# A planned attention kernel: more shifted copies by transfer, a constant row from VectorE, an epsilon add on GpSimd, other thresholds of the planner

## The chip, the cores and the metric

One core of one Trainium2 chip runs the kernel. Five engines work from instruction streams of their own: TensorE (PE; its weight loads stand apart as PEld), VectorE (DVE), ScalarE (ACT), GpSimd (POOL) and SyncE (SP, which here only issues transfers). The metric is the time of one execution on the device in microseconds, as the median of the timed runs; lower is better.

## What is computed

Four layers on one sequence of 2048 rows of 512 numbers (bf16): two attention layers (A), each followed by a linear-attention layer (B), with a layer norm ahead of each and a residual around it. A has 32 query heads of width 16 that share one key and one value head.

```python
def _A_ref(x, wq, wk, wv, wo):
    q = (x @ wq).reshape(B, S, H, Dh).transpose(0, 2, 1, 3)
    k = x @ wk
    v = x @ wv
    scores = jnp.einsum("bhqd,bkd->bhqk", q, k) * (Dh ** -0.5)
    p = _softmax(scores, axis=-1)
    o = jnp.einsum("bhqk,bkd->bhqd", p, v)
    return o.transpose(0, 2, 1, 3).reshape(B, S, H * Dh) @ wo

def _B_ref(x, wqkv, wo):
    q, k, v = split(x @ wqkv)
    phi = lambda t: jnp.where(t > 0, t + 1, jnp.exp(t)) + 1e-6
    pq, pk = phi(q), phi(k)
    kv = jnp.einsum("bhsd,bhse->bhde", pk, v)
    den = jnp.einsum("bhqd,bhd->bhq", pq, pk.sum(2))[..., None] + 1e-6
    o = jnp.einsum("bhqd,bhde->bhqe", pq, kv) / den
    return o.transpose(0, 2, 1, 3).reshape(B, S, D) @ wo

x = A_x
x = x + _A_ref(_layernorm(x), A_wq, A_wk, A_wv, A_wo)
x = x + _B_ref(_layernorm(x), B_wqkv, B_wo)
x = x + _A_ref(_layernorm(x), A_wq, A_wk, A_wv, A_wo)
x = x + _B_ref(_layernorm(x), B_wqkv, B_wo)
```

## The kernel before

**The order is planned ahead.** The program does not write its instructions down in order. While it is built, a class `Planner` plays an event simulation: each operation has a duration, a latency and a priority, an engine takes the ready operation with the lowest priority number, and the order in which they were taken is written out as that engine's instruction stream. On the chip each engine works through its stream strictly in order and waits at semaphores. So a duration or a threshold in the planner costs nothing by itself; it changes which instructions there are, and in which order they stand.

**Blocks of attention.** The 2048 rows are 16 tiles of 128. A layer A has 16 query tiles x 2 halves of the heads x 16 key tiles x 4 row groups: 2048 blocks of 128 keys x 512 query columns, so 4096 in the two layers. For each block PE computes scores into a PSUM bank (L958; two to four blocks run side by side in PE's rows), somebody takes the exponential, and PE multiplies the result with V (L1012; up to four blocks side by side in PE's columns). The exponential has two ways:

- **ACT**: one activation (L1134) over two or three banks, bf16 into a buffer (PT, or borrowed space in xnT and OBB). The block needs one product with V.
- **DVE**: a scaled score becomes, by one add and a maximum into int16 (`dve_take`, L1215), the bits of a bf16 power of two with a linear mantissa. To smooth it, the block is used four times (`NSH = 4`), shifted by 0, 1, 2 and 3 quarters of an octave and weighted: four products with V, the shifted weights standing in VW. Four blocks form a chunk of 128x2048 in a buffer (FB, or borrowed space in OBB, sacc, xn, wq and wo2), and three further buffers take the shifted copies. A shift is one int16 add over the chunk (`dve_shifts`, L1263).

**Copies by transfer.** One of the three copies of a chunk, that for shift `DSH = 1`, can be made without DVE. A generator `prime` loads a free buffer with a constant row from DRAM (`cst`, named shift_row; a transfer of 512 KB from SP's queue, L1283), keeps up to `NPRE` such buffers, and `dma_shift` issues from POOL a transfer that adds the chunk onto the buffer (`accum_op=ALU.add`, L1292). `dve_shifts` uses it if the chunk is full, a primed buffer is there, the segment is not among the last `DMIN`, and the planner's transfer path, `pl.dmaq`, is less than `DQ` us behind. The path is modelled as one queue: an adding transfer occupies it for `DXF`, a load for `DPF`, and each lands `DTAIL` later; `PGEN` is the time for which POOL is held by an issue. A load starts only while more than `FBP` buffers are free.

**Thresholds.** `TUNE[0]` is put over the defaults when the first A layer begins, `TUNE[2]` when the second does, and what neither names stays as it was left. `BLO`, `BLT`, `BLS` and `DXB` are limits on DVE's planned backlog for giving it a block; `CHT` and `ENDL` say how far ahead of ACT's place a block for DVE must lie; `AHEAD` and `FBS` hold a chunk's copies back while buffers are short; `FBO` is how many buffers must stay free before a new chunk is opened; `STICK` is the margin in priority by which PE stays with its present kind of matmul (rows or columns); `LAG` is a look-ahead of DVE and ACT in the B layers. Where PE has nothing ready, short matmuls without use are inserted (fillers: `fill`, L1057).

**Layer norm.** `ln_tile` computes for each tile mean and variance (L810, L811), adds epsilon (ve, L812, on DVE), raises to -0.5 on POOL (rs, L814) and normalizes on DVE (xn, L817). xn is transposed by PE, or for tiles that are not urgent by a transposing transfer from SP's queue (L736, planned at `DTL = 4.0` us). VW comes from POOL (L861). In program order POOL's stream holds these small operations and the issues of the adding transfers, one behind the other; SP's holds loads, transposes and stores.

**The constant row** is made at the start by a POOL memset of a whole FB buffer (L691), and its first partition is stored to DRAM (L692).

Of the kernel before, what the change touches and what calls it, by code (L numbers as in the profile page):

```python
# [7 lines left out]
FP32 = mybir.dt.float32  # L8
I16 = mybir.dt.int16
ACTF = mybir.ActivationFunctionType  # L10
ALU = mybir.AluOpType

PE, AC, DV, PO, SP = "pe", "act", "dve", "pool", "sp"
ENGS = (PE, AC, DV, PO, SP)

P = 128
S, D, H, DH = 2048, 512, 32, 16
T = S // P
# [325 lines left out]
class Seg:  # L344
# [11 lines left out]
    def take(self, js, back=False):  # L356
# [22 lines left out]
LAG = 0.15  # L379
# [16 lines left out]
BLS = 1.4  # L396
BLO = 5.0
DXB = 2.0
BLT = 2.5
# [11 lines left out]
ENDL = 12  # L411
NSH = 4
# [6 lines left out]
FBO = 2  # L419
FBS = 4  # L420
AHEAD = 20
CHT = 19
PSH = False
STICK = 1.5
# [3 lines left out]
DSH = 1  # L428
DMIN = 4
NPRE = 2  # L430
PGEN = 1.1
DPF = 2.5
DXF = 4.5
DTAIL = 2.5
DQ = 4.0
FBP = 6
TUNE = {0: {"FBS": 5, "AHEAD": 15, "LAG": 0.15, "ENDL": 12, "FBO": 0, "BLO": 7.0, "DXB": 1.6, "BLT": 3.2},
        2: {"FBS": 3, "DXB": 1.6, "ENDL": 9, "BLS": 1.0}}


def bass_interleave_layers__grouped_kv_mqa__linear_attn_block__prompt_kernel(
# [12 lines left out]
    op = pl.op  # L454
    sb = nc.alloc_sbuf_tensor
# [18 lines left out]
    xn = sb("xn", [P, NXN, D], BF16)  # L474
    st = sb("st", [P, T, 2, 6], FP32)
    mv = sb("mv", [P, T, 2], FP32)
    ve = sb("ve", [P, T], FP32)
    rs = sb("rs", [P, T], FP32)
    mhalf = sb("mhalf", [P, 1], FP32)
    ident = sb("ident", [P, P], BF16)  # L480
    mask8 = sb("mask8", [P, 8, 17], BF16)
# [11 lines left out]
    NFB = 12  # L493
    FB = sb("FB", [P, NFB, CHB * 512], BF16)
# [179 lines left out]
    def pool_op(fn, writes, reads=(), dur=0.2, prio=0.0):  # L674
        return op({PO: (dur, fn)}, reads=reads, writes=writes, prio=prio)
# [10 lines left out]
    cst = nc.dram_tensor("shift_row", (1, CHB * 512), I16, kind="Internal").ap()  # L686

    def fb_keys(i):
        return [("FB", i, h) for h in range(CHB)]

    pool_op(lambda e: e.memset(FB[:, NFB - 1, :].bitcast(I16), DSH * 128 // NSH), fb_keys(NFB - 1), dur=1.2, prio=8.0)  # L691
    op({SP: (0.54, lambda e: e.dma_start(cst, FB[0:1, NFB - 1, :].bitcast(I16)))}, reads=fb_keys(NFB - 1), writes=["cst"], prio=8.0, lat=2.5, dma=True)  # L692
    pool_op(lambda e: e.memset(kmask[:, 1:2], KSC), ["kmask"], dur=0.1)
    for j in range(4):
        for r, v in ((0, KSC), (1, 0.0)):
# [42 lines left out]
    def until(*keys):  # L738
        for k in keys:
            yield ("ops", pl.ws(k))  # L740
# [60 lines left out]
    def ln_tile(L, t, prio, far=False, crit=False):  # L801
# [6 lines left out]
        else:  # L808
            n = 1
            op({DV: (0.6, lambda e: e.bn_stats(st[:, t, 0, :], x_sb[:, t, :]))}, reads=[("x", t)], writes=[("st", t)], prio=prio, lat=0.13)  # L810
        op({DV: (0.09, lambda e: e.bn_aggr(mv[:, t, :], st[:, t, 0:n, :]))}, reads=[("st", t)], writes=[("mv", t)], prio=prio, lat=0.13)  # L811
        op({DV: (0.07, lambda e: e.tensor_scalar(out=ve[:, t:t + 1], in0=mv[:, t, 1:2], scalar1=1e-5, scalar2=None, op0=ALU.add))},  # L812
           reads=[("mv", t)], writes=[("ve", t)], prio=prio, lat=0.16)
        op({PO: (0.55, lambda e: e.tensor_tensor(out=rs[:, t:t + 1], in0=ve[:, t:t + 1], in1=mhalf[:], op=ALU.pow))},  # L814
           reads=[("ve", t), "mhalf"], writes=[("rs", t)], prio=prio - 9.0)
        i = yield ("acq", xn_pool, prio)
# [132 lines left out]
    def run_a(L):  # L949
# [324 lines left out]

        def prime():
            yield ("flag", ("K", L, T - 1))
            yield from until("cst")
            while state["si"] < len(segs) - DMIN:
                if len(primed) >= NPRE or len(fb_pool.free) <= FBP or fb_pool.wait:
                    yield ("sleep", 0.2)  # L1280
                    continue
                g_ = yield ("acq", fb_pool, 9.0)
                o = op({SP: (0.54, lambda e, g_=g_: e.dma_start(fbs[g_].bitcast(I16), cst.to_broadcast([P, CHB * 512])))}, reads=["cst"], writes=fb_keys(g_), prio=9.0,  # L1283
                       lat=0.2, dma=True, behind=guest(L, "FB", g_), xfer=(DPF, DTAIL))
                primed.append((g_, o))
            while primed:
                g_, o = primed.pop()
                pl.give_after(fb_pool, g_, [o])
# [607 lines left out]
```

## Time and profile before

| what | value |
|---|---|
| timed runs, median (lowest to highest) | 1501.41 us (1501.35 to 1501.43), 3 runs |
| profiled execution, on the device | 1502.7 us |
| its span in the profile | 1501.0 us |
| granted clock of TensorE | 1.00 |
| busy: PE, DVE, ACT, POOL | 94%, 95%, 97%, 11% |
| transfers | 128.76 MB, mean 86 GB/s |

The span runs from the first to the last instruction of the profiled execution; what lies around it makes its device time 1.7 us longer. Busy time is the union of an engine's instructions. On ACT and DVE an instruction's record overlaps the start of the next one, so that the mean of a group is longer than the time for which it holds the engine. Fillers on PE count as busy. The stages, by the share of busy time: 0 to 50 us start, 50 to 700 the first attention layer (with parts of the first B layer inside it), 700 to 850 the rest of the first B layer and the start of the second attention layer, 850 to 1450 the second attention layer, then the end.

### The profile page before, as it was taken

To read this page: it belongs to the slowest core of one execution; us is meant where nothing else is said; L and a number is where in the kernel's file an instruction comes from. 1 tells how busy PE (TensorE), PEld (TensorE's weight loads), DVE (VectorE), ACT (ScalarE), POOL (GpSimd) and SP (SyncE) were. 2 spreads that over 40 slices of the span, in tenths; PEclk is the share of its full clock that TensorE was granted. 3 is DMA by queue.
4 is the path that set the end of the run, shared out by engine and by line. 5 is a ranking of instruction groups with operands and counts; after the bars stand their busy time and mean duration, and the time that the engine had idled before them with its cause. 6 is when DMAs were issued, how large, how long until landed. Compare 5 with 4: busy or idle time off the path is not lost.

```text
span 1501.0 us, 36621 instructions
## 1 busy us (share of the span) xinstructions
PE 1418.2 (94%) x14634; PEld 514.3 (34%) x14745; DVE 1426.3 (95%) x2684; ACT 1453.6 (97%) x1519; POOL 167.2 (11%) x230
## 2 busy tenths in 40 slices
PE   7999999999999999999999999999999999999998
PEld 4433333332232233323744332333332332323335
DVE  8899999999999999998867799999999999999997
ACT  7999999999999999999799999999999999999996
POOL 5100101101010100000111101111111111100001
PEclk9999999999999999999999999999999999999999
DMA  4624533433443434001000124446464674552001
GB/s 107 176 65 114 124 65 92 106 89 78 104 104 66 92 93 89 30 15 58 2 2 1 30 51 106 111 120 152 116 152 111 151 157 108 134 131 58 16 2 57
DMA packets 71738, 128.76 MB, mean 86 GB/s; under 512 B 37521, under 2 KB 44177, under 8 KB 71570
## 3 DMA queue, kind: packets, MB, share of 16 engines
q0 software_dynamic: 14832, 54.01, 19.2%
q1 hardware_dynamic: 56738, 72.41, 16.4%
q8 instruction: 119, 1.95, 0.5%
q14 instruction: 49, 0.40, 0.1%
HBM read 62.42 MB, written 2.10 MB: 43 GB/s over the span
## 4 chain that ended last, share of the span: by engine, by line
PE 35%; DVE 33%; ACT 24%; issue 7%; POOL 0%; ACTq 0%; POOLq 0%
ACT PT L1134 16%; PE ps L1012 13%; DVE FB L1215 12%; PE ps L958 11%; DVE FB L1263 8%; PE ps L730 4%; ACT xnT L1134 3%; ACT OBB L1134 3%; PE ps L891 2%; DVE OBB L1215 2%; PE ps L1057 2%; PE ps L1365 1%; DVE sacc L1215 1%; DVE xn L1215 1%; DVE wq L1263 1%
## 5 line engine op out<-in xcount | busy, mean ns | idle before, releaser
L1134 ACT ACTIVATE PT<-ps 128x1024 bf16<-128x1024 f32 (+1 forms) x951 | 1016.4, 1179 | 6.3 <-PE ps L1012 3.0
L958 PE MATMUL ps<-QT,KM 32*128 32x512 bf16 x4096 | 536.5, 385 | 43.0 <-ACT PT L1134 18.0
L1215 DVE TENSOR_SCALAR FB<-ps 128x512 int16<-128x512 f32 x790 | 521.0, 682 | 5.6 <-PE ps L958 4.4
L1012 PE MATMUL ps<-FB,VW 128*32 128x512 bf16 x3126 | 501.5, 385 | 9.5 <-ACT PT L1134 3.1
L1012 PE MATMUL ps<-PT,V 128*32 128x512 bf16 x2108 | 431.4, 386 | 2.2 <-ACT PT L1134 1.3
L958 PEld LDWEIGHTS ps<-QT,KM 32*128 32x128 bf16 x4096 | 134.1, 91 | 442.2 <-ACT PT L1134 216.2
L1134 ACT ACTIVATE xnT<-ps 128x1024 bf16<-128x1024 f32 (+1 forms) x241 | 267.8, 1158 | 3.7 <-PE ps L1012 2.0
L1263 DVE TENSOR_SCALAR FB<-FB 128x2048 int16<-128x2048 int16 (+1 forms) x354 | 237.2, 678 | 0.3
L1134 ACT ACTIVATE OBB<-ps 128x1024 bf16<-128x1024 f32 (+1 forms) x167 | 190.1, 1170 | 1.2 <-PE ps L958 0.5
L1012 PEld LDWEIGHTS ps<-FB,VW 128*32 128x32 bf16 x3126 | 123.3, 94 | 146.9 <-issue 86.0
L1012 PE MATMUL ps<-xnT,V 128*32 128x512 bf16 x530 | 144.5, 385 | 0.7 <-ACT xnT L1134 0.3
L1057 PE MATMUL ps<-QT,V 128*32 128x512 bf16 (+6 forms) x571 | 132.1, 316 | 0.8 <-DVE FB L1215 0.4
L1012 PEld LDWEIGHTS ps<-PT,V 128*32 128x32 bf16 x2108 | 104.8, 94 | 70.5 <-issue 44.4
L1012 PE MATMUL ps<-OBB,V 128*32 128x512 bf16 x372 | 108.9, 385 | 1.5 <-ACT PT L1134 0.5
L1292 POOL DMA_DIRECT2D FB<-FB x56 | 52.1, 930 | 422.0 <-DVE FB L1215 247.6
L814 POOL TENSOR_TENSOR rs<-ve,mhalf 128x1 f32<-128x1 f32 x64 | 46.0, 722 | 463.1 <-DVE ve L812 462.9
L1012 PE MATMUL ps<-xn,VW 128*32 128x512 bf16 x256 | 69.3, 384 | 0.1
L1012 PE MATMUL ps<-sacc,VW 128*32 128x512 bf16 x246 | 68.2, 384 | 0.7 <-ACT PT L1134 0.6
L730 PE MATMUL ps<-wqkv,xnT 128*128 128x512 bf16 (+1 forms) x209 | 65.5, 369 | 3.0 <-issue 1.7
L1057 PEld LDWEIGHTS ps<-QT,V 128*32 128x32 bf16 x571 | 44.4, 95 | 63.2 <-issue 43.3
L1012 PE MATMUL ps<-wq,VW 128*32 128x512 bf16 x244 | 64.2, 384 | 1.2 <-ACT PT L1134 1.1
L1012 PE MATMUL ps<-OBB,VW 128*32 128x512 bf16 x240 | 58.5, 385 | 3.2 <-ACT PT L1134 1.4
(206 smaller groups left out, 1662.2 us busy)
## 6 DMA issues: line engine op xcount, KB each, us to landing
FB<-shift_row SPq DMA_DIRECT2D x81, 512.0 KB, 4.6
FB<-FB POOLq DMA_DIRECT2D x56, 512.0 KB, 5.0
wo<-shift_row SPq DMA_DIRECT2D x10, 512.0 KB, 4.3
FB<-sacc POOLq DMA_DIRECT2D x8, 512.0 KB, 5.1
FB<-xn POOLq DMA_DIRECT2D x6, 512.0 KB, 5.4
wo<-FB POOLq DMA_DIRECT2D x6, 512.0 KB, 4.9
xn<-shift_row SPq DMA_DIRECT2D x6, 512.0 KB, 4.5
FB<-wo POOLq DMA_DIRECT2D x5, 512.0 KB, 4.9
```

Source lines behind the costliest of these rows:

```text
L730: return e.matmul(dst, lhsT=l, rhs=r, start=(k == 0), stop=(k == len(pairs) - 1))
L814: op({PO: (0.55, lambda e: e.tensor_tensor(out=rs[:, t:t + 1], in0=ve[:, t:t + 1], in1=mhalf[:], op=ALU.pow))}, reads=[("ve", t), "mhalf"] ...
L891: ins = e.matmul(dst[:, g * P:(g + 1) * P], lhsT=lhs(g, k), rhs=rhs(k), start=(k == 0), stop=(k == FT - 1))
L958: return e.matmul(bank(b), lhsT=KM[r, sg.par, kt * P:(kt + 1) * P], rhs=QT[r, sg.t, :], start=True, stop=True)
L1012: ins = e.matmul(ps[32 * j:32 * j + 32, ACC * 512:(ACC + 1) * 512], lhsT=V[:, kt, :] if w is None else VW[:, kt, w, :], rhs=ap, start=(k = ...
L1057: o = op({PE: (n / 2400.0, lambda e: e.matmul(ps[32 * j:32 * j + 32, b * 512:b * 512 + n], lhsT=V0[:], rhs=QT[:, sg.t, 0:n], start=st, sto ...
L1134: ex = op({AC: (0.051 + 0.4267 * n, lambda e, n=n, s_=s_, p_=p_: e.activation(pts[p_][:, 0:n * 512], ps[:, s_ * 512:(s_ + n) * 512], ACTF. ...
L1215: o = op({DV: (0.602, lambda e: e.tensor_scalar(out=dst.bitcast(I16), in0=bank(b), scalar1=VB, scalar2=VLO, op0=ALU.add, op1=ALU.max))}, w ...
L1263: o = op({en: (du, lambda e, w=w, g_=g_: e.tensor_scalar(out=fbs[g_][:, 0:n].bitcast(I16), in0=fbs[f_][:, 0:n].bitcast(I16), scalar1=float ...
L1292: o = op({PO: (PGEN, lambda e: e.dma_start(fbs[g_].bitcast(I16), fbs[f_].bitcast(I16), accum_op=ALU.add))}, reads=fb_keys(f_), writes=fb_k ...
L1365: o = op({PE: (0.12, lambda e, c=c: e.transpose(ps[:, b * 512 + c * P:b * 512 + (c + 1) * P], src[:, c * P:(c + 1) * P], identF[:]))}, rea ...
```

## The change

The planner's figures for a transfer are set to other values (an issue on POOL 0.95 us, 2.2 us of the path for a load, 2.8 for an adding transfer, 1.6 to land), and the thresholds for both A layers are replaced. The constant row is made by a DVE memset of one partition once the sixteenth key tile of the first layer is there, and stored then. Epsilon is added on POOL. The two small tensors rs and ve change places in memory. In the changed program's streams there are 203 adding transfers and 207 loads of the constant row, where there were 103 and 107. Lines between the removed memset and `prime` move up by two, those behind it down by two.

```diff
-PGEN = 1.1
-DPF = 2.5
-DXF = 4.5
-DTAIL = 2.5
+PGEN = 0.95
+DPF = 2.2
+DXF = 2.8
+DTAIL = 1.6
 DQ = 4.0
-FBP = 6
-TUNE = {0: {"FBS": 5, "AHEAD": 15, "LAG": 0.15, "ENDL": 12, "FBO": 0, "BLO": 7.0, "DXB": 1.6, "BLT": 3.2},
-        2: {"FBS": 3, "DXB": 1.6, "ENDL": 9, "BLS": 1.0}}
+FBP = 4
+TUNE = {0: {"CHT": 13, "FBO": 1, "FBS": 3, "BLO": 3.5, "DXB": 1.2, "DMIN": 4, "STICK": 2.5, "LAG": 0.05, "BLT": 3.2, "FBP": 2},
+        2: {"DXB": 2.0, "BLT": 2.8, "FBP": 2, "LAG": 0.0, "ENDL": 9, "NPRE": 2, "AHEAD": 10, "DMIN": 2, "FBS": 2, "BLO": 5.0}}
...
+    rs = sb("rs", [P, T], FP32)
     ve = sb("ve", [P, T], FP32)
-    rs = sb("rs", [P, T], FP32)
...
-    pool_op(lambda e: e.memset(FB[:, NFB - 1, :].bitcast(I16), DSH * 128 // NSH), fb_keys(NFB - 1), dur=1.2, prio=8.0)
-    op({SP: (0.54, lambda e: e.dma_start(cst, FB[0:1, NFB - 1, :].bitcast(I16)))}, reads=fb_keys(NFB - 1), writes=["cst"], prio=8.0, lat=2.5, dma=True)
...
-        op({DV: (0.07, lambda e: e.tensor_scalar(out=ve[:, t:t + 1], in0=mv[:, t, 1:2], scalar1=1e-5, scalar2=None, op0=ALU.add))},
-           reads=[("mv", t)], writes=[("ve", t)], prio=prio, lat=0.16)
+        op({PO: (0.1, lambda e: e.tensor_scalar(out=ve[:, t:t + 1], in0=mv[:, t, 1:2], scalar1=1e-5, scalar2=None, op0=ALU.add))},
+           reads=[("mv", t)], writes=[("ve", t)], prio=prio - 9.0, lat=0.08)
...
         def prime():
             yield ("flag", ("K", L, T - 1))
+            if L == 0:
+                row = FB[0:1, NFB - 1, :].bitcast(I16)
+                op({DV: (0.6, lambda e: e.memset(row, DSH * 128 // NSH))}, writes=fb_keys(NFB - 1), prio=1.0)
+                op({SP: (0.54, lambda e: e.dma_start(cst, row))}, reads=fb_keys(NFB - 1), writes=["cst"], prio=1.0, lat=2.5, dma=True)
             yield from until("cst")
```

## The prediction

> **What bounds the kernel now.** The page comes first: the busy shares, then the span in slices.
>
> ```profile
> span 1501.0 us, 36621 instructions
> PE 1418.2 (94%) x14634; PEld 514.3 (34%) x14745; DVE 1426.3 (95%) x2684; ACT 1453.6 (97%) x1519; POOL 167.2 (11%) x230
> ...
> DVE  8899999999999999998867799999999999999997
> ACT  7999999999999999999799999999999999999996
> ...
> DMA  4624533433443434001000124446464674552001
> ```
>
> Three engines are nearly full, so the shares do not yet say which one sets the end. The table by stages does; I cut it where the digits change.
>
> ```profile
> 0.00:50.00 50.00, 39.12 (x406) 20.58 (x409) 38.62 (x114) 39.97 (x47) 20.89 (x60) 1.00 0.55 158
> 50.00:700.00 650.00, 617.28 (x6357) 204.49 (x6402) 647.75 (x1164) 645.82 (x651) 58.38 (x61) 1.00 0.35 82
> ...
> 750.00:850.00 100.00, 94.31 (x957) 44.14 (x968) 67.54 (x154) 96.76 (x90) 12.50 (x26) 1.00 0.01 2
> 850.00:1450.00 600.00, 572.54 (x5887) 187.31 (x5925) 596.16 (x1079) 596.56 (x617) 67.55 (x72) 1.00 0.46 106
> 1450.00:1501.00 51.00, 46.63 (x455) 26.80 (x456) 37.70 (x73) 36.54 (x61) 4.18 (x4) 1.00 0.13 43
> ```
>
> Each row has PE, PEld, DVE, ACT and POOL busy, the granted clock (1.00 throughout), the DMA share and GB/s. In the two attention stages (1250 us together) DVE is busy 1243.9 us and ACT 1242.4 us: both are full, because both compute exponentials out of PSUM and the planner hands the next block to whichever is free. PE is at 95% there, but part of that is filler:
>
> ```profile
> 50.00:700.00 650.00, 63.84 (x292) 22.63 (x292) 1.00 0.35 82
> ...
> 850.00:1450.00 600.00, 56.11 (x235) 18.26 (x235) 1.00 0.46 106
> ```
>
> This is the same table for the filler line L1057 alone: 120 us of PE's time are matmuls that only fill idle time. With the 60 us that PE stands idle in the two stages, some 180 of 1250 us are slack. So the end is set by the work of ACT and DVE together; whatever takes work off both at once shortens the two stages one for one, until PE has to wait for something.
>
> **The change part by part.** Counted in the two programs' instruction lists (no time is in them): on POOL 203 adding transfers instead of 103, and on SP 207 constant-row loads instead of 107. DVE loses 67 shifts of 2048 elements (710 to 643) and three of 1024, loses the 64 epsilon adds, and takes 42 more blocks at L1215 (1086 to 1128). ACT loses those 42 blocks: 1067 to 1117 activations of two blocks, 292 to 244 of three, two of one.
>
> ACT's price. A row's mean overlaps the next instruction, so I take the time of the whole line and the difference of the two forms.
>
> ```profile
> L1134 ACT ACTIVATE PT<-ps 128x1024 bf16<-128x1024 f32 x745 | 753.9, 1085 | 4.4 <-PE ps L958 2.2 <-PE ps L1012 1.4
> L1134 ACT ACTIVATE PT<-ps 128x1536 bf16<-128x1536 f32 x206 | 307.4, 1517 | 2.0 <-PE ps L1012 1.6 <-PE ps L958 0.2
> ```
> ```profile
> sum 1501.00, ACT 1388.97; mean ACT 231.49
> ```
>
> The second fence is the total of L1134 over all windows. A third block costs 1517 - 1085 = 432 ns; then (1388.97 - 292 x 0.432) / 1359 = 0.929 us for two blocks, 1.361 for three and 0.497 for one. Change: 50 x 0.929 - 48 x 1.361 + 2 x 0.497 = -17.9 us. Two QT copies come over from DVE at about 0.5 us each: -17 us.
>
> DVE's price, by the starts of successive instructions:
>
> ```profile
> 1219.89 1.28 DVE L1215 TENSOR_SCALAR FB<-ps 128x512 int16<-128x512 f32 x2
> ...
> 1221.09 0.28 DVE L1454 TENSOR_SCALAR phE<-phE 128x512 bf16<-128x512 bf16 x1
> ...
> 1230.78 0.14 DVE L812 TENSOR_SCALAR ve<-mv 128x1 f32<-128x1 f32 x1
> 1230.84 0.68 DVE L1263 TENSOR_SCALAR wq<-FB 128x2048 int16<-128x2048 int16 x1
> 1231.44 0.68 DVE L1263 TENSOR_SCALAR FB<-FB 128x2048 int16<-128x2048 int16 x1
> ```
>
> Two blocks start 1.20 us before the next instruction, 0.60 each; a shift holds the engine 0.60, an epsilon add 0.06. Change: +42 x 0.60 - 67 x 0.60 - 3 x 0.3 - 64 x 0.06 = -19.7 us; the two QT copies that left give -1.2. The new 1x2048 memset lies between 0.6 us (a shift has as many elements) and 2.4 (512 elements from PSUM take 0.6); I take 1. Sum: -20 us. ACT and DVE shrink by nearly the same, so neither is left behind as the other's limit, and the smaller, -17, goes into the sum.
>
> PE gets 126 more block products at L1012. They run four to a wave; waves follow each other in 0.21 us (by the starts below), so 126 / 4 x 0.21 = +6.6 us. Against the 180 us of slack this costs nothing; without that cover it would be these 6.6 us.
>
> ```profile
> 1230.18 0.59 PE L1012 MATMUL ps<-PT,V 128*32 128x512 bf16 x3
> ...
> 1230.39 0.60 PE L1012 MATMUL ps<-FB,VW 128*32 128x512 bf16 x6
> ...
> 1230.61 0.38 PE L1012 MATMUL ps<-xnT,V 128*32 128x512 bf16 x1
> ```
>
> The transfers. What holds for one, and for the path as a whole:
>
> ```profile
> q0 software_dynamic: 14832, 54.01, 19.2%
> ```
> ```profile
> 118.00:126.00 8.00, 7.75 (x99) 2.91 (x97) 8.00 (x16) 8.00 (x9) 0.35 (x1) 1.00 0.40 133
> ```
>
> q0 carries the adding transfers alone: 19.2% of 1501 us over 103 is 2.80 us of the sixteen engines each. From 118 to 126 us two constant rows are loaded and nearly nothing else: 0.40 x 8 / 2 = 1.6 us each. A hundred more pairs are 440 us. The two stages now use 0.35 x 650 + 0.46 x 600 = 504 us; 944 of 1250 is 75%. It fits, but with little room: transfers will meet more often. How late is a transfer that meets another? Time from issue to landing, of the adding transfers in the whole run and in the densest stretch, 1100 to 1360 us, and of the transposes likewise:
>
> ```profile
> DMA to landing us min/median/max: 4.5/5.0/10.7
> ...
> DMA to landing us min/median/max: 4.5/4.9/10.7
> ...
> DMA to landing us min/median/max: 2.4/2.5/5.7
> ...
> DMA to landing us min/median/max: 2.4/3.7/5.7
> ```
>
> The planner charged an adding transfer that meets no other 1.1 + 0.3 + 4.5 + 2.5 = 8.4 us from issue to landing; it now charges 0.95 + 0.3 + 2.8 + 1.6 = 5.65. The median of 5.0 keeps 0.65 us in hand, but the cover of some 3 us that swallowed nearly every late one is gone. The order on PE is fixed, so a copy that lands after its place stops PE, and behind it the next scores for both ACT and DVE. Today no wait of PE on an adding transfer is among the rows that the view of waits gives. Transposes are still charged 4.0 us, and in the dense stretch their median has already gone from 2.5 to 3.7.
>
> I cannot price that from a row. Below, it is 0: what is late falls into PE's slack. Above: if a fourth of 203 transfers land 0.5 us past their place and nothing hides it, 25 us. The trace is nearer to the lower end (the median is early, PE has 14% of slack, ACT has a second set of banks to work from), so I take 5 us.
>
> [...]
>
> ```profile
> L1292 POOL DMA_DIRECT2D FB<-FB x15: 859/862/1027, 1099.8 to 1357.4; - x15
> L1292 POOL DMA_DIRECT2D FB<-sacc x4: 862/1054/1354, 1128.8 to 1300.5; - x4
> ```
> ```profile
> 850.00:1450.00 600.00, 217.69 (x326) 1.00 0.46 106
> ```
>
> Above, the issues of the dense stretch (shortest, median, longest ns); below, DVE's time in shifts (L1263) in the whole stage. Most issues last 0.86 us although DVE shifts for 36% of the time; some last 0.5 longer. By the rows this is inside the 5 us; taken for every transfer it is a rival below.
>
> Start of the kernel. The POOL memset of the constant row goes away, and this is what it did:
>
> ```profile
> 4.18 0.55 POOL L814 TENSOR_TENSOR rs<-ve,mhalf 128x1 f32<-128x1 f32 x1
> 4.70 0.36 POOL L711 TENSOR_SCALAR_AFFINE_SELECT mask<-mask 128x136 bf16<-128x136 bf16 x1
> 5.01 1.80 POOL L691 MEMSET FB<- 128x2048 int16 x1
> ```
> ```profile
> 4.77 2.18 DVE L817 TENSOR_SCALAR xn<-x_sb,mv,rs 128x512 bf16<-128x512 bf16 x1 [0.68 <-POOL rs L814]
> ```
> ```profile
> L817 DVE TENSOR_SCALAR xn<-x_sb,mv,rs 128x512 bf16<-128x512 bf16 x64 | 27.9, 436 | 3.3 <-POOL rs L814 3.1
> ```
>
> The first tile's xn lasts 2.18 us instead of 0.44 and ends just after the memset: it was held by it, on the chain that starts everything. That gives back 1.7 us. Against it, in the changed order POOL does the epsilon add and a mask select (0.36) ahead of this rs: 0.4 to 0.8 later. Net -1. Elsewhere the epsilon add saves DVE's instruction on the few critical tiles (the first, tile 15 of each layer, tiles 0 and 1 of the third layer) and costs POOL between 0.1 (its 128x1 memsets) and 0.56 (rs) us; six tiles, -1 to +2 us, taken as 0. In the attention stages it also stands behind transfers that wait for their data, but those tiles are needed late. The row is now stored after the sixteenth K tile, so the first layer's transfers begin some 3 us later: one or two fewer, already in the count of 203.
>
> Sum: -17 (ACT and DVE) - 1 (start) + 5 (late transfers) = -13. The profiled execution lasted 1502.7 us (span 1501.0), the timed runs' median is 1501.41; I predict the median: 1488.5.
>
> **The rivals.** *Late transfers eat the gain.* If at 75% load the transfers pile up, as the transposes' 3.7 against 2.5 and the maximum of 10.7 suggest, PE's fixed order stops again and again: a quarter late by 0.5 us is +25, and the time 1501 - 18 + 25 = 1508. It decides from 18 / 203 = 0.09 us of unhidden delay per transfer, which is little. Against it: no such stop in the dense stretch, where ACT was busy 258.98 of 260 us.
>
> ```profile
> 1100.00:1360.00 260.00, 247.33 (x2595) 80.53 (x2610) 257.31 (x465) 258.98 (x273) 35.65 (x38) 1.00 0.59 135
> ```
>
> *VectorE's shifts hold up GpSimd.* Every second issue half a microsecond longer (1354 against 862 ns), unhidden: 203 / 2 x 0.5 = +50 us, and if half of that falls into slack 1508 as well. [...] The many issues at 862 speak against it.
>
> *All of it arrives.* Nothing is late: 1501 - 18 = 1483, or 1480 where DVE's 20 us set it.
>
> *The work moves, the time does not.* The freed time of ACT and DVE turns into waits for PE, which keeps its mode switches and gets 126 products more: within 3 us of 1501. Against it stand the 120 us of filler.
>
> **How the numbers follow.** The forecast (part of the gain lost) 45%, with its own range 1483 to 1496; all of it 20%; late transfers 20% (4 of it so mild that it ends below 1498); shifts that hold up GpSimd 5% (1 below 1498); no change 10% (8 within 3 us, 2 above). What a measurement of this kernel tells from no change is about 0.2%, 3 us. Faster: 45 + 20 + 4 + 1 = 70%; same 8%; slower 16 + 4 + 2 = 22%. Range for 8 in 10: from 1480 (all of it) to 1512 (the far side of the late transfers).
>
> **What would show it.** ACT's line L1134 down by 17 to 18 us in total, L1215 and L1263 together by about 16; DMA share in both attention stages near 0.75; xn of the first tile under 0.6 us. For the forecast, ACT's idle time in the two stages rises from 8 us to no more than 13. Wrong: waits of PE on transfers, or landings whose median goes past 5.65 us, with ACT idle for 20 us or more.

## The result, and the profile after

| | before | after |
|---|---|---|
| timed runs, median (lowest to highest) | 1501.38 us (1501.11 to 1501.43) | 1550.43 us (1540.01 to 1555.17) |
| ratio to before, 95% interval | | 1.0318 (1.0264 to 1.0371) |
| profiled execution / its span | 1502.7 / 1501.0 us | 1540.01 / 1538.3 us |
| granted clock, mean over the span | 1.000 | 0.988 (0.976 to 0.983 in the three others) |

The changed kernel is 49 us slower, and its runs scatter by 15 us where those of before lie within 0.3 us (on the chips of the later runs some executions of before reached 1508 us). The page of the changed kernel, its busy shares and the slices that answer to those shown of before:

```profile
span 1538.3 us, 37193 instructions
PE 1446.6 (94%) x14750; PEld 508.1 (33%) x14750; DVE 1411.7 (92%) x2593; ACT 1444.9 (94%) x1523; POOL 277.9 (18%) x393
...
DVE  7999999998998889999776899989999999899997
ACT  8999999998998989999799999989999999899996
...
DMA  4878887986887788402000489888678787787501
...
q0 software_dynamic: 29232, 106.44, 37.2%
...
issue 26%; PE 24%; DVE 20%; DMA 12%; ACT 11%; POOL 6%; POOLq 0%; ACTq 0%; SPq 0%; DVEq 0%
```

DVE and ACT have less to do than before (1426.3 and 1453.6 us then), but the eights in their rows of slices are new: in slices in which nothing but attention runs, both stand idle for a tenth and more. The last line is the chain that ended last, by engine: transfers hold 12% of it. The stages of the changed kernel (PE, PEld, DVE, ACT and POOL busy, granted clock, DMA share, GB/s; the second stage ends 25 us later than before):

```profile
50.00:700.00 650.00, 607.35 (x6185) 192.20 (x6181) 617.10 (x1089) 620.99 (x634) 116.99 (x129) 0.99 0.75 171
850.00:1475.00 625.00, 593.93 (x6000) 191.97 (x5999) 591.24 (x1056) 593.87 (x619) 112.43 (x131) 0.98 0.75 174
```

ACT's idle time is 29 us in the first stage and 31 in the second, 60 instead of 8. The DMA share is 0.75 in both, as counted, and the clock is no longer 1.00. What PE waited for (us in total, times, longest), and below it the source views of the adding transfers and of the transposes (who waited for them; shortest, median and longest time from issue to landing):

```profile
PE ps L1010 <- DMA FB<-FB: 19.3, 13, 2.3
...
PE ps L728 <- DMA xnT<-xn: 7.4, 4, 3.4
...
PE ps L1010 <- DMA FB<-OBB: 4.7, 5, 2.3
```
```profile
  PE ps L1010: 35.5, 31
...
DMA to landing us min/median/max: 4.4/6.4/11.3
```
```profile
  PE ps L728: 7.4, 4
...
DMA to landing us min/median/max: 2.4/4.0/8.2
```

PE stood still for 35.5 us at the products with transferred copies and for 7.4 us at the matmuls that read transposed xn, 43 us in all; before, there was no such wait. The median landing of an adding transfer, 6.4 us, is past the 5.65 that the planner now allows. One of these stops, as a table of 2 us windows of the changed kernel, with the instructions around it on PE and on SP's queue:

```profile
356.00:358.00 2.00, 1.89 (x22) 0.51 (x17) 2.00 (x4) 2.00 (x3) 0.00 (x0) 1.00 1.40 68
358.00:360.00 2.00, 0.13 (x1) 0.00 (x0) 1.61 (x3) 1.42 (x2) 0.78 (x1) 1.00 0.69 132
360.00:362.00 2.00, 0.52 (x2) 0.14 (x2) 0.00 (x0) 0.00 (x0) 0.07 (x1) 0.76 1.02 285
362.00:364.00 2.00, 2.00 (x13) 0.33 (x11) 0.37 (x1) 0.37 (x1) 0.00 (x0) 0.50 1.09 246
364.00:366.00 2.00, 2.00 (x20) 0.41 (x17) 1.60 (x3) 1.67 (x2) 0.00 (x0) 0.50 0.91 305
366.00:368.00 2.00, 2.00 (x15) 0.42 (x11) 0.70 (x2) 1.02 (x1) 0.00 (x0) 0.53 0.64 231
368.00:370.00 2.00, 2.00 (x22) 0.76 (x19) 1.80 (x3) 1.83 (x3) 0.84 (x1) 1.00 0.13 45
```
```profile
357.63 0.50 PE L1055 MATMUL ps<-QT,V 128*32 128x384 bf16 x2
...
361.48 1.01 PE L728 MATMUL ps<-wqkv,xnT 128*128 128x512 bf16 x2 [3.36 <-DMA xnT<-xn]
```
```profile
352.35 0.32 SPq L1285 DMA_DIRECT2D FB<-shift_row  x1
353.10 1.19 SPq L734 DMA_TRANSPOSE xnT<-xn  x1
354.40 0.53 SPq L1285 DMA_DIRECT2D FB<-shift_row  x1
```

A transpose issued at 353.10 stands between two loads of the constant row; PE goes on at 361.48, 8.4 us after the issue, where the plan gave it 4.0. PE has waited 3.36 us; DVE and ACT run dry less than 2 us after PE has stopped (1.61 and 1.42 us busy from 358 to 360, 0.00 from 360 to 362). The DMA share of so short a window can stand above 1, and nothing here rests on it. Then comes what was in none of my terms: PE is busy again, but the granted clock is 0.76, 0.50, 0.50 and 0.53 in the four windows from 360 to 368, and ACT and DVE, which live on PE's scores, are busy for some 3 of these 8 us. These four windows lack (0.24 + 0.50 + 0.50 + 0.47) x 2 = 3.4 us of full clock. So PE lost 3.4 us by this stop itself and another 3.4 behind it.

Not every stop brings this. The granted clock of the changed kernel falls to half eight times within the run, five times for 3.4 us and three times for 6.8, and each time a wait of PE for a transfer stands just ahead. But there were 35 such waits. Two of them, and the windows behind each:

```profile
253.27 0.39 PE L1010 MATMUL ps<-xn,VW 128*32 128x512 bf16 x2 [2.31 <-DMA FB<-FB]
...
1335.52 0.39 PE L1010 MATMUL ps<-FB,VW 128*32 128x512 bf16 x1 [1.44 <-DMA FB<-FB]
```
```profile
253.00:255.00 2.00, 1.73 (x20) 0.58 (x21) 0.95 (x3) 0.96 (x2) 0.00 (x0) 1.00 1.01 215
255.00:257.00 2.00, 1.96 (x21) 0.82 (x20) 2.00 (x4) 2.00 (x4) 0.57 (x1) 1.00 0.17 33
...
1336.00:1338.00 2.00, 2.00 (x19) 0.42 (x18) 1.72 (x3) 1.39 (x2) 0.00 (x0) 0.81 0.53 104
1338.00:1340.00 2.00, 2.00 (x14) 0.79 (x10) 0.81 (x3) 1.20 (x2) 0.00 (x0) 0.50 0.03 8
```

A stop of 2.31 us left the clock at 1.00, and one of 1.44 us was followed by half of it. So the length of a stop does not decide this alone; what else does is open.

The whole account, from the rows above: 43 us of waits and (1 - 0.988) x 1538 = 18 us of missing clock, 61 us. Two experiments below check that sum.

### The profile page after: what moved, and what is told of

It is laid out like the page before. It is cut to its first block, busy times and chain, and to the rows that moved or that the text cites. A ratio compares the mean times of both kernels' runs of the same rounds, so it can differ in the third digit from the quotient of the medians.

```text
span 1538.3 us, 37193 instructions
## 1 busy us (share of the span) xinstructions
PE 1446.6 (94%) x14750; PEld 508.1 (33%) x14750; DVE 1411.7 (92%) x2593; ACT 1444.9 (94%) x1523; POOL 277.9 (18%) x393
## 3 DMA queue, kind: packets, MB, share of 16 engines
q0 software_dynamic: 29232, 106.44, 37.2%
## 4 chain that ended last, share of the span: by engine, by line
issue 26%; PE 24%; DVE 20%; DMA 12%; ACT 11%; POOL 6%; POOLq 0%; ACTq 0%; SPq 0%; DVEq 0%
PE ps L1010 9%; DVE FB L1213 8%; ACT PT L1132 7%; PE ps L956 7%; DMA FB<-FB 4%; DVE FB L1261 4%; PE ps L728 3%; POOL FB L1294 3%; PE ps L889 2%; ACT xnT L1132 1%; DMA FB<-OBB 1%; DMA OBB<-FB 1%; ACT OBB L1132 1%; DVE xn L1213 1%; PE ps L1055 1%
## 5 line engine op out<-in xcount | busy, mean ns | idle before, releaser
L1132 ACT ACTIVATE PT<-ps 128x1024 bf16<-128x1024 f32 (+1 forms) x953 | 1006.9, 1157 | 42.6 <-PE ps L956 40.6
L1010 PE MATMUL ps<-FB,VW 128*32 128x512 bf16 x3248 | 541.3, 388 | 23.8 <-DMA FB<-FB 8.4
L956 PE MATMUL ps<-QT,KM 32*128 32x512 bf16 x4096 | 539.8, 388 | 22.4 <-ACT PT L1132 10.7
L1213 DVE TENSOR_SCALAR FB<-ps 128x512 int16<-128x512 f32 x780 | 513.1, 681 | 39.3 <-PE ps L956 38.1
L1010 PE MATMUL ps<-PT,V 128*32 128x512 bf16 x2090 | 444.6, 388 | 7.0 <-DMA FB<-FB 2.0
L1132 ACT ACTIVATE xnT<-ps 128x1024 bf16<-128x1024 f32 (+1 forms) x237 | 254.5, 1114 | 11.7 <-PE ps L956 10.8
L1261 DVE TENSOR_SCALAR FB<-FB 128x2048 int16<-128x2048 int16 x305 | 206.0, 681 | 0.3
L1132 ACT ACTIVATE OBB<-ps 128x1024 bf16<-128x1024 f32 (+1 forms) x173 | 190.5, 1135 | 6.8 <-PE ps L956 6.5
L1294 POOL DMA_DIRECT2D FB<-FB x97 | 94.0, 969 | 401.9 <-DVE FB L1213 359.9
L1055 PE MATMUL ps<-QT,V 128*32 128x512 bf16 (+5 forms) x447 | 108.2, 314 | 0.3 <-DVE xn L1213 0.3
L728 PE MATMUL ps<-wqkv,xnT 128*128 128x512 bf16 (+1 forms) x272 | 89.1, 387 | 8.2 <-DMA xnT<-xn 7.4
L1010 PE MATMUL ps<-wo,VW 128*32 128x512 bf16 x260 | 78.0, 388 | 3.6 <-DMA FB<-FB 1.3
L810 POOL TENSOR_SCALAR ve<-mv 128x1 f32<-128x1 f32 x64 | 26.1, 410 | 289.5 <-DVE mv L809 288.0
L1010 PE MATMUL ps<-OBB,VW 128*32 128x512 bf16 x248 | 71.4, 390 | 1.1 <-DMA OBB<-FB 0.5
```

What stands on the lines that cost most here:

```text
L728: return e.matmul(dst, lhsT=l, rhs=r, start=(k == 0), stop=(k == len(pairs) - 1))
L810: op({PO: (0.1, lambda e: e.tensor_scalar(out=ve[:, t:t + 1], in0=mv[:, t, 1:2], scalar1=1e-5, scalar2=None, op0=ALU.add))}, reads=[("mv", ...
L956: return e.matmul(bank(b), lhsT=KM[r, sg.par, kt * P:(kt + 1) * P], rhs=QT[r, sg.t, :], start=True, stop=True)
L1010: ins = e.matmul(ps[32 * j:32 * j + 32, ACC * 512:(ACC + 1) * 512], lhsT=V[:, kt, :] if w is None else VW[:, kt, w, :], rhs=ap, start=(k = ...
L1055: o = op({PE: (n / 2400.0, lambda e: e.matmul(ps[32 * j:32 * j + 32, b * 512:b * 512 + n], lhsT=V0[:], rhs=QT[:, sg.t, 0:n], start=st, sto ...
L1132: ex = op({AC: (0.051 + 0.4267 * n, lambda e, n=n, s_=s_, p_=p_: e.activation(pts[p_][:, 0:n * 512], ps[:, s_ * 512:(s_ + n) * 512], ACTF. ...
```

## The experiments

One table holds what the profiles of all kernels say. Share: DMA share of the windows 50 to 700 and 850 to 1450 us (for the changed kernel to 1475). Landing: median and longest time from issue to landing, of the adding transfers that the kernel uses and of the transposes. Waits: time for which PE waited for adding transfers and for transposes. These and the clock are those of one profiled execution, the time is the median of the runs. The ratio is to the kernel before on the same chip, with its 95% interval.

| kernel | adding transfers | share | landing, adds | landing, transposes | waits of PE, us | clock | time, us | ratio |
|---|---|---|---|---|---|---|---|---|
| before | 103 | 0.35, 0.46 | 5.0, 10.7 | 2.5, 5.7 | 0, 0 | 1.000 | 1501.4 | |
| after | 203 | 0.75, 0.75 | 6.4, 11.3 | 4.0, 8.2 | 35.5, 7.4 | 0.988 | 1550.4 | 1.032 (1.026 to 1.037) |
| e13_quarter_both | 203 short | 0.29, 0.29 | 3.1, 6.5 | 2.5, 5.4 | 0, 0 | 1.000 | 1481.4 | 0.985 (0.982 to 0.988) |
| e14_quarter_adds | 203 short | 0.44, 0.44 | 3.4, 6.6 | 2.5, 4.4 | 0.3, 0 | 1.000 | 1482.5 | 0.985 (0.983 to 0.988) |
| e6_unused_load | 103 + 103 unused | 0.72, 0.91 | 8.4, 17.8 | 4.8, 19.7 | 20.5, 43.0 | 0.972 | 1590.4 | 1.056 (1.053 to 1.059) |
| e11_unused_loads | 103 | 0.51, 0.64 | 6.1, 12.5 | 3.1, 7.8 | 12.0, 4.7 | 0.993 | 1526.4 | 1.016 (1.014 to 1.018) |
| e12_unused_adds | 103 + 103 unused | 0.59, 0.75 | 5.8, 15.2 | 3.2, 10.4 | 6.4, 11.7 | 0.989 | 1530.9 | 1.020 (1.018 to 1.021) |
| e2_copies_later | 204 | 0.75, 0.80 | 6.3, 10.7 | 3.7, 9.8 | 12.6, 7.6 | 0.990 | 1535.8 | 1.020 (1.016 to 1.024) |
| e3_transposes_later | 200 | 0.73, 0.75 | 6.6, 10.5 | 3.4, 10.5 | 52.3, 0 | 0.980 | 1582.3 | 1.051 (1.045 to 1.058) |
| e4_both_later | 202 | 0.77, 0.78 | 6.7, 12.1 | 3.9, 10.2 | 23.4, 4.0 | 0.986 | 1527.4 | 1.016 (1.010 to 1.022) |
| e8_more_fillers | 209 | 0.75, 0.81 | 6.5, 11.0 | 3.7, 10.8 | 46.6, 4.9 | 0.978 | 1558.7 | 1.037 (1.033 to 1.041) |
| e1_small_edits | 105 | 0.39, 0.45 | 5.0, 10.6 | 2.5, 6.4 | 0.3, 2.2 | 0.998 | 1509.0 | 1.004 (1.003 to 1.005) |
| e5_few_meet | 127 | 0.49, 0.50 | 5.3, 8.3 | 2.5, 6.4 | 3.8, 0 | 0.997 | 1507.0 | 1.003 (1.001 to 1.004) |
| e7_old_figures | 145 | 0.54, 0.58 | 5.1, 8.9 | 2.5, 6.7 | 0, 3.8 | 0.990 | 1502.1 | 1.001 (0.999 to 1.003) |
| e10_margins_144 | 144 | 0.52, 0.57 | 5.2, 10.6 | 2.5, 6.3 | 1.8, 0 | 0.998 | 1497.9 | 0.997 (0.996 to 0.998) |
| e9_margins_126 | 126 | 0.47, 0.50 | 5.1, 9.5 | 2.5, 8.4 | 0.5, 0 | 0.999 | 1494.6 | 0.995 (0.994 to 0.996) |

A changed figure or threshold of the planner gives another order of all instructions, so such runs are not pure subtractions. Five runs change no order: e13 and e14 keep that of the changed kernel, e6, e11 and e12 that of the kernel before. The verdict rests on these.

**The same order with short transfers.** Every adding transfer, and every load but the first into a buffer, moves a quarter of its columns, so that three of the four blocks of each transferred copy are left out (of the long lines only the calls are shown):

```diff
+                w = 512 if g_ in whole else CHB * 512
+                whole.add(g_)
-  e.dma_start(fbs[g_].bitcast(I16), cst.to_broadcast([P, CHB * 512]))
+  e.dma_start(fbs[g_][:, 0:w].bitcast(I16), cst[:, 0:w].to_broadcast([P, w]))
-  e.dma_start(fbs[g_].bitcast(I16), fbs[f_].bitcast(I16), accum_op=ALU.add)
+  e.dma_start(fbs[g_][:, 0:512].bitcast(I16), fbs[f_][:, 0:512].bitcast(I16), accum_op=ALU.add)
```

> The changed kernel's own order, instruction for instruction, but every adding transfer moves 128x512 numbers instead of 128x2048, and every load of a constant row too, except the first load into each buffer. So three of four blocks of a transferred copy hold a wrong shift: that part of the computation is left out, while all the work of ACT, DVE and PE is the changed kernel's. Theory A (late transfers and the clock drops behind them are all that went wrong): the DMA share of the stages falls from 0.75 to below 0.35, adding transfers land at a median under 4.5 us, PE waits under 2 us on transfers, the granted clock is 0.995 or more, ACT's idle time in the two stages falls from 60 us to under 20, and the time is 1480 to 1492, about the 1485 that the counted work gives. Theory B (the new order itself costs, by its waits between PE, ACT and DVE): no transfer is late, and the time still stays above 1500.

> As the run with both transfers short, but only the adding transfers are short (128x512 of 128x2048; three of four blocks of a transferred copy then hold a wrong shift); the loads of the constant row are whole. Theory A with sharing (what counts is the load of the sixteen engines together): the share is near 0.40 to 0.45, adding transfers land at a median under 5 us against the 5.65 that the plan gives them, PE waits under 5 us on transfers and the time is 1482 to 1500. If loads alone hold up the short adding transfers (a queue of the loads in front of them): waits of 15 us and more, and a time above 1510.

Measured: 1481.41 us, and 1482.46 with the loads whole. The stages of e13 and the landing of its adding transfers:

```profile
50.00:700.00 650.00, 617.14 (x6435) 201.24 (x6485) 641.90 (x1138) 646.15 (x663) 117.14 (x131) 1.00 0.29 59
850.00:1450.00 600.00, 576.67 (x6046) 194.87 (x6090) 593.24 (x1072) 590.72 (x624) 110.58 (x129) 1.00 0.29 58
```
```profile
DMA to landing us min/median/max: 2.6/3.1/6.5
```

PE waits for no transfer, the clock is 1.00, and ACT is idle for 13 us in the two stages. Instruction for instruction the order is that of the changed kernel, so the order costs nothing and without late transfers it is worth 1501 - 1481 = 20 us. The profiled execution of the changed kernel lies 1540.0 - 1481.4 = 59 us above it: the account from the waits and the clock gave 61. Theory B, that the new order costs by its own waits, falls. In e14, with whole loads, the share is 0.44 and PE waits 0.3 us in all, so 207 loads alone don't do it; whole adding transfers beside short loads were not run.

**The order of before, with transfers that nobody uses.** Behind each load stands a load of the same size into scratch memory in DRAM, behind each adding transfer an add of 512 KB onto that scratch (e6); e11 adds the loads alone, e12 the adds alone (and eight loads that fill the scratch).

```diff
+    for q, made in ((SP, loads), (PO, adds)):
+        order = []
+        for o in pl.order[q]:
+            order.append(o)
+            if o.isdma and o.xfer:
...
+                if q == SP:
+                    d = plain(q, lambda e, i=i: e.dma_start(scr[i], cst.to_broadcast([P, CHB * 512])), pl.ws("cst"), o.end)
+                else:
+                    d = plain(q, lambda e, i=i: e.dma_start(scr[i], wqkv[:].rearrange("p f c -> p (f c)")[:, 0:CHB * 512].bitcast(I16), accum_op=ALU.add), pl.ws("wqkv"), o.end)
+                order.append(d)
```

> The kernel before with its order on PE, DVE and ACT untouched; behind each of its loads and adding transfers stands an unused one of the same size on the same queue (constant row to a scratch in DRAM, 512 KB of wqkv added onto it), for whose data no engine waits. Theory A2: the used adds land later (median from 5.0 to 6.5 us or more), but the order of before expects them 8.4 us after the issue, so PE's waits on them stay between 3 and 25 us with some clock drops, time 1503 to 1535. Theory B (the traffic slows the engines themselves): L1134, L1215 and L1263 take longer per instruction, time over 1540. If neither, within 3 us of 1501.

> The kernel before, its order untouched, with 107 unused loads of the constant row to a scratch in DRAM behind the used ones and no unused adds. If the loads on SP's queue are what holds up transposes (same queue) and adds: transposes' median from 2.5 to 4 us or more, PE's waits on transposes over 10 us, time 1510 to 1550. If the loads are harmless: within 5 us of 1502.

> The kernel before, its order untouched, with 103 unused adding transfers (wqkv onto a scratch in DRAM) behind the used ones on POOL's queue and no unused loads but eight that fill the scratch. If adds hold up each other and everything else on the sixteen engines: used adds land after 7 us or more in the median, PE's waits on adds over 10 us, time 1515 to 1560. If adds are harmless to transposes: their median stays under 3 us and time is within 10 us of 1502.

Measured: 1590.36, 1526.40 and 1530.88 us; e6 went past what I expected, because transposes were hit harder than adding transfers. e11 and e12 lie in their ranges of time, but by less delay than I had expected: transposes at a median of 3.1 us, not 4, with 4.7 us of waits in e11; adding transfers at 5.8 us, not 7, with 6.4 us of waits in e12. Landing in e6, of the used adding transfers and, below, of the transposes:

```profile
DMA to landing us min/median/max: 4.7/8.4/17.8
```
```profile
DMA to landing us min/median/max: 2.4/4.8/19.7
```

Work and order are those of before; only the transfers doubled, and 88 us came with them. (The unused issues also take time in the streams of POOL, 1.27 us each in the mean, and SP; a landing is counted from its own issue and is free of that, a wait of PE need not be.) The account holds: in e6 63.5 us of waits and 0.028 x 1593 = 45 of clock, 108, against 93 that its profiled execution took more than before; in e11 17 + 11 = 28 against 22, in e12 18 + 17 = 35 against 33. It is somewhat too high each time, presumably because part of a wait falls into slack. The loads come from SP's queue and delay POOL's adding transfers (median 5.0 to 6.1 us); the adds come from POOL and delay SP's transposes (2.5 to 3.2, longest 10.4). So it isn't only the queue of one engine that is held up. The page of e6 counts the time of both queues as shares of the same sixteen engines (q0, which carries the adds, 37.2% of the span, q1 29.6%); whether a transfer is held up in these engines or in the memories behind them, no run here tells apart. The speed of ACT and DVE was not touched: a pair of blocks on ACT took 1082 ns in e6 and 1085 before, a shift on DVE 680 in both.

**A later place for the copies, for the transposes, for both.** The changed kernel with other landing times in the plan; e2 has the first edit, e3 the second, e4 both, and in e4 `TUNE[0]` has `CHT` 17 in place of 13 and `TUNE[2]` `FBO` 0:

```diff
-DTAIL = 1.6
+DTAIL = 3.2
```
```diff
-DTL = 4.0
+DTL = 6.0
```

> The changed kernel with DTAIL 3.2 instead of 1.6, so that PE's order expects each adding transfer 1.6 us later; transposes stay planned at 4.0 us; 204 adding transfers. Theory A: PE's waits on adding transfers fall from 35 us to under 8; waits on transposes (8 us) and one or more clock drops stay; time 1500 to 1525. Theory B (the load of the transfers itself slows the kernel, wherever their results are used): time stays at 1535 or more with a DMA share near 0.8 in the attention stages.

> The changed kernel with DTL 6.0 instead of 4.0, so that PE's order expects transposes 2 us later; adding transfers planned as in the changed kernel; 200 of them. Theory A: PE's waits on transposes fall from 8 us to under 2 and the drops they cause go, waits on adding transfers stay at 25 us or more; time 1520 to 1545. Theory B: 1535 or more. If the transposes alone are the cause: under 1510.

> The changed kernel with DTAIL 3.2 and DTL 6.0, and two thresholds set so that the block counts stay near (CHT 17 for the first attention layer, FBO 0 for the second); 202 adding transfers. Theory A: PE's waits on all transfers under 6 us in all, at most one clock drop (mean clock 0.997 or more), ACT idle near the 40 us of before; time 1485 to 1500, so faster than before. Theory B: as many transfers, DMA share still near 0.8, so 1530 or more.

Measured: 1535.76, 1582.26, 1527.41 us, each past the range I had for the theory. The direction of the waits was right: 35.5 us on adding transfers became 12.6 with 1.6 us more of margin, 7.4 on transposes became 0 with 2 us more. But e3 put 52.3 us on the adding transfers, and e4 still has 23.4. A margin somewhat above the median did not reach the longest landings, 10 to 12 us at a share of 0.75 to 0.80. The times of e2 and e3 also lie in the range that I had written for theory B, a load that slows the kernel wherever its results are used. Against it stand the speeds of ACT and DVE in e6, and the account: in the profiled executions, measured from the 1481 us of e13, waits and clock make up 84 of 84 us in e3 and 49 of 51 in e4. In e2 they make up only 36 of 54, and what the orders of these kernels cost by themselves was not separated.

**More fillers.** The changed kernel, with a higher rate of matmul columns up to which the planner puts in fillers (209 adding transfers in the order that results):

```diff
-WORK = 5000
+WORK = 6000
```

> The changed kernel with WORK 6000 instead of 5000, so that PE's planned idle time holds 228 thousand columns of fillers instead of 165 thousand; 209 adding transfers, landing planned as in the changed kernel. If the halved clock is a separate loss that busier PE windows prevent: fewer than 4 clock drops instead of 8, waits on transfers as before (25 us or more), time 1515 to 1535. If a stop of PE brings the drop whatever surrounds it: 6 drops or more and 1540 to 1565.

Measured: 1558.67 us, clock 0.978. The filler line took 143.4 us instead of 108.2, and the clock is no better than the 0.976 to 0.988 of the changed kernel: 0.022 x 1558 = 34 us of it are missing in the profiled execution, against 18. The time is that of the second of the two cases that I had written down. What I make of it, without a run that shows it alone: where PE stands at a semaphore, the fillers behind it in the stream stand too.

**The small edits alone.** The kernel before with the row from VectorE, epsilon on GpSimd and rs and ve exchanged, none of the figures and thresholds.

```diff
-    pool_op(lambda e: e.memset(FB[:, NFB - 1, :].bitcast(I16), DSH * 128 // NSH), fb_keys(NFB - 1), dur=1.2, prio=8.0)
...
+                op({DV: (0.6, lambda e: e.memset(row, DSH * 128 // NSH))}, writes=fb_keys(NFB - 1), prio=1.0)
...
-        op({DV: (0.07, lambda e: e.tensor_scalar(out=ve[:, t:t + 1], in0=mv[:, t, 1:2], scalar1=1e-5, scalar2=None, op0=ALU.add))},
+        op({PO: (0.1, lambda e: e.tensor_scalar(out=ve[:, t:t + 1], in0=mv[:, t, 1:2], scalar1=1e-5, scalar2=None, op0=ALU.add))},
```

> The kernel before with only the small edits: constant row by VectorE, epsilon on GpSimd, rs and ve exchanged; thresholds and transfer figures of before, so about as many adding transfers (105 against 103). Theory A (late landings against PE's fixed order, made longer by the halved clock): the small edits are innocent, time within 5 us of 1501, granted clock 1.00, no wait of PE on an adding transfer of more than 3 us in all; xn of the first tile under 1 us instead of 2.18. Theory C (the epsilon add in POOL's queue delays the layer norms): 1510 or more, with DVE xn waiting for POOL rs more than 8 us in all.

Measured: 1508.95 us, 7 us above before and so past my 5. The timeline of PE in e1 has a reason for 5.6 of the 9 us by which the profiled execution (1511.71 us) is longer:

```profile
458.17 0.47 PE L728 MATMUL ps<-wqkv,xnT 128*128 128x512 bf16 x1 [2.16 <-DMA xnT<-xn]
```

In the new order one transpose, issued 1.1 us behind an adding transfer, lands after its place: PE stops for 2.2 us, and behind it the granted clock is 0.58, 0.50, 0.50 and 0.71 in the four windows of 2 us from 458 to 466: half the clock for some 6.8 us, 3.4 lost. A single meeting was enough, in a stage with a share of 0.39 where before had 0.35. The rest is open, and the rival of this run, the epsilon add that delays the layer norms, is not excluded here: DVE's xn waited 12.3 us for rs, past the 8 that I had named, and 3.1 before. In the changed order it did not keep e13, with 9.0 us of these waits, from 1481 us.

**Fewer transfers that meet, and the old margins.** e5 loads only when the planned path has been empty for 1 us; e7 is the changed kernel with the figures of before; e10 and e9 have these figures, more time for transposes and thresholds that ask for fewer transfers.

```diff
-                if len(primed) >= NPRE or len(fb_pool.free) <= FBP or fb_pool.wait:
+                if len(primed) >= NPRE or len(fb_pool.free) <= FBP or fb_pool.wait or pl.dmaq > pl.now + DGAP:
```

That is e5, with `DGAP` -1.0, `NPRE` 1 in both layers, `DTAIL` 2.4, `DQ` 0.5 and `DTL` 6.0. For e7, e9 and e10:

```diff
-PGEN = 0.95
-DPF = 2.2
-DXF = 2.8
-DTAIL = 1.6
+PGEN = 1.1
+DPF = 2.5
+DXF = 4.5
+DTAIL = 2.5
```

e10 has `DTL` 6.5 besides, and in `TUNE[2]` `NPRE` 1 and `CHT` 17. e9 has `DTL` 6.5, `DQ` 2.0 and

```diff
+TUNE = {0: {"CHT": 15, "FBO": 1, "FBS": 3, "BLO": 3.5, "DXB": 1.2, "DMIN": 4, "STICK": 2.5, "LAG": 0.05, "BLT": 2.8, "FBP": 2, "ENDL": 9},
+        2: {"DXB": 1.2, "BLT": 3.2, "FBP": 2, "LAG": 0.15, "ENDL": 12, "NPRE": 1, "AHEAD": 15, "DMIN": 2, "FBS": 4, "BLO": 5.0, "STICK": 1.5}}
```

> The changed kernel with transfers kept apart: a constant row is loaded only when the planned path has been empty for 1 us, one primed buffer instead of two (NPRE 1), an adding transfer only when the path is less than 0.5 us behind (DQ 0.5), DTAIL 2.4, DTL 6.0; 127 adding transfers are left. Theory A2 (a transfer that meets others shares the sixteen engines with them, and loads issued early hold up the adds that PE waits for): landing of the adds back to a median of 5.2 us or less with a maximum under 8, PE's waits on transfers under 4 us in all, mean clock 0.998 or more, time 1493 to 1505. Theory T (the new thresholds order PE's work badly whatever the transfers do): 1515 or more with ACT idle over 60 us and few waits on transfers.

> The changed kernel with the transfer figures of before (PGEN 1.1, DPF 2.5, DXF 4.5, DTAIL 2.5) and all else as changed: the new thresholds plan 145 adding transfers, each expected 8.4 us after its issue. Theory A2: PE's waits on transfers under 10 us, at most two clock drops, time 1494 to 1512. Theory T: 1520 or more.

> The changed kernel with the figures of before and DTL 6.5, DQ as in the changed kernel, NPRE 1 and CHT 17 in the second attention layer; 144 adding transfers. Theory A2: against e7 with as many transfers the waits on transposes (4 us there) are gone, waits on adds under 4 us, 1493 to 1502. If the margins do not hold at this load: 1504 or more.

> The changed kernel with margins for every transfer: the figures of before (an add expected 8.4 us after its issue), transposes expected after 6.5 us (DTL 6.5), an adding transfer only while the planned path is less than 2 us behind (DQ 2.0), and thresholds chosen for these figures; 126 adding transfers. Theory A2: no wait of PE on a transfer over 1 us, clock 0.998 or more, landing of the adds 5.2 us in the median; the work saved by 23 more transfers and fewer planned gaps shows: 1490 to 1499, so faster than before. If 126 transfers still stop PE: 1503 or more.

Measured: 1507.00, 1502.12, 1497.88 and 1494.63 us. e5 missed its range by 2 us, with 3.8 us of waits left; the others came as expected. Giving back the figures alone (e7) takes away all waits on adding transfers and 48 us: it lowers their number to 145 and gives each 8.4 us. (The clock of 0.990 in the table is that of its profiled execution of 1511.23 us, whose page has 7 in the clock's second slice, 37.7 to 75.5 us, and 9 in all others: at least 0.2 x 37.7 = 7.5 us of clock are missing there. In the whole run PE waited for two transfers, transposes both, 2.2 and 1.6 us. What brought this drop is open; eight of its ten runs lie between 1499.9 and 1506.4.) e9 beats the kernel before by 0.5% (0.37 to 0.64). Its stages and the landing of its adding transfers:

```profile
50.00:700.00 650.00, 612.58 (x6323) 201.25 (x6373) 642.16 (x1142) 644.49 (x649) 78.84 (x92) 1.00 0.47 108
850.00:1450.00 600.00, 569.03 (x5909) 187.50 (x5957) 597.32 (x1073) 594.10 (x613) 77.28 (x92) 1.00 0.50 116
```
```profile
DMA to landing us min/median/max: 4.4/5.1/9.5
```

With 126 transfers the share is 0.47 and 0.50, the median is back at 5.1 us, and a margin of 8.4 covers all but one that stops PE, for 0.5 us.

## Why the prediction was wrong

**The step that failed** is the term for late transfers: "The trace is nearer to the lower end (the median is early, PE has 14% of slack, ACT has a second set of banks to work from), so I take 5 us", with 25 as its upper bound. It came to 59 us in the profiled execution (1540.0 against 1481.4 with the same order and short transfers), and to 69 by the medians. The prediction's own sign of being wrong came in full: waits of PE on transfers, a median landing past 5.65 us, ACT idle for more than 20. Three things stood in that sentence:

- *The median is early.* I compared the 5.0 us of a half empty path with a plan of 5.65 for a path at 0.75. At that load the median itself is 6.4. The one row that showed the trend, the transposes' 3.7 us in the dense stretch, was quoted and not used for the sum.
- *PE has slack.* The slack is filler, and it stands in the same ordered stream. A stop at one semaphore presumably holds it up too (no run shows that alone), and e8, with a third more of it, gained nothing.
- *ACT has a second set of banks.* In the windows shown it lasted less than 2 us. That may bridge a stop of average length (35.5 us over 31 waits), but not the slow stretch behind it; ACT's idle time of 60 us is what counts. How much of a single short stop the banks hide was not measured.

**A term was missing.** I took the granted clock of 1.00 as given. Behind eight of its 35 waits for transfers PE had half the clock for 3.4 or 6.8 us, 18 us of the 59 in the profiled execution, and more in the others: (1 - 0.976) x 1553 = 37 us in the slowest, 19 more than in the profiled one, where the time is 15 longer. The kernel before is not free of this: in the later runs its executions of 1503.3 us and more have a clock of 0.995 to 0.998, the shorter ones 1.000.

**A victim was missing.** The median landing of a transpose went from 2.5 to 4.0 us. Transposes were mentioned and given no price; four stops cost 7.4 us of waits, the longest of all among them.

**The rivals.** *Late transfers eat the gain* had the mechanism, PE's fixed order, and the right sign; its price, a quarter late by 0.5 us, was too small: 31 waits on adding transfers lasted 1.1 us on average, and the clock was not in it. *Shifts that hold up GpSimd* is not what happened. In the trace of before the 25 of 103 issues (L1292) that took more than 0.95 us all overlap a shift (L1263), and the 24 that overlap none took 0.91 us at most; but POOL is busy for 117 us of the first stage in e13 as in the changed kernel, with the same 203 issues beside the same shifts, and e13 takes 1481 us. *All of it arrives*, 1483, is about what the order would have given: 1481 was measured once the transfers were short (20 us less than before, of which the rows below show 15 on ACT; the other 5 were not traced). *No change* falls with it.

**What was right.** In e13, where no stop disturbs the rows, L1132 is 1374.0 us in total against 1389.0 before, -15 where -17.9 was counted, and L1213 with L1261 1173.5 against 1188.1, -15 where -16 was counted. In the changed kernel itself L1132 is only 9 us shorter (1379.9), presumably, though no run shows it alone, because an activation that had to wait doesn't overlap the one ahead of it. The start of the changed kernel, on DVE and POOL:

```profile
5.09 0.45 DVE L815 TENSOR_SCALAR xn<-x_sb,mv,rs 128x512 bf16<-128x512 bf16 x1 [1.21 <-POOL rs L812]
...
40.52 1.76 DVE L1277 MEMSET FB<- 1x2048 int16 x1 [0.36 <-issue]
```
```profile
L810 POOL TENSOR_SCALAR ve<-mv x64: 202/222/1181, 4.0 to 1505.9; 128x1 f32<-128x1 f32 x64
```

The first xn takes 0.45 us instead of 2.18 and ends at 5.54 instead of 6.95: -1.4 against -1. The memset on DVE took 1.76 us where I had taken 1, inside its bounds; epsilon costs POOL a median of 0.22 us. The DMA share of 0.75 was exact. So the work and the load were counted right, and the load's consequence was not.

## What to carry over

Where instructions stand in a fixed order and the end is set by keeping engines fed, a transfer's place must be planned by the slow tail of landings at the load that the change creates (here 11.3 us), not by the median at the load of today (5.0). A wait in front of TensorE cost its own length here, 43 us in all, and in eight of 35 cases a stretch at half the clock, 18 us in all; more slack in the same stream (e8) did not pay for it. To price late transfers before a change, put unused ones of the same size into the present order: here that gave the sign, though not the size (88 us against 49).

## What the runs showed of the hardware

- **Half a clock after a short stop, but not after every one.** A stop of 3.36 us brought the windows at 0.50 shown above; one of 2.16 us in e1 brought as much (0.58, 0.50, 0.50 and 0.71), and one of 1.44 us in the changed kernel was followed by as much (0.81, 0.50, 0.50 and 0.50). The eight stretches of the changed kernel lasted 3.4 us (five) and 6.8 us (three). Stops of 2.31 and 2.29 us in the changed kernel brought none (1.00 in the windows behind them), and in e7 at least 7.5 us of clock are missing in one slice, where the two waits for transfers in the whole run were 2.2 and 1.6 us.
- **Landing grew with the load of the sixteen engines, whoever issued.** Median of a 512 KB adding transfer: 5.0 us at shares of 0.35 and 0.46, 6.1 at 0.51 and 0.64, 6.4 at 0.75, 8.4 at 0.72 and 0.91 (but 5.8 at 0.59 and 0.75, so the share alone does not set it); the longest went from 10.7 to 17.8, that of a transpose from 5.7 to 19.7.
